# Two spectra kept in HBM in blocks of four frequencies: long runs for the stores, short runs for the loads

## The chip, the cores and the metric

The kernel runs on one NeuronCore of a Trainium2 chip. The metric is the device time of one execution in microseconds (us). A core has a matrix engine (PE, with its weight loads on PEld), a vector engine (DVE), an activation engine (ACT), a general engine (POOL), and a sync engine (SP) that issues nearly all DMAs here. PE reads SBUF and writes PSUM; only DMAs reach HBM. Sixteen DMA engines, which all queues share, carry the transfers.

## The reference

A long causal convolution by FFT over 8 sequences of 5696 tokens with 128 channels, followed by a mixture of 8 experts in which each token goes to one expert:

```python
L = 2 * S                                   # S = 5696
Xf = np.fft.rfft(x, n=L, axis=1)            # x: 8 x 5696 x 128
Hf = np.fft.rfft(h, n=L, axis=0)
y = np.fft.irfft(Xf * Hf[None], n=L, axis=1)[:, :S]
x = y.reshape(B * S, D)
logits = x @ w_gate                         # 8 experts
expert_idx = np.argmax(logits, axis=1)
probs = softmax(logits); gate_w = probs[expert_idx]
for e in range(E):                          # tokens of expert e
    out[mask] = gate_w[mask] * (relu(xe @ w1[e]) @ w2[e])
```

All of it is float32.

## The kernel before

The FFT is done in steps that are matrix products. The 8 sequences are split into three groups of 2, 3 and 3 (`SPLIT`). A group goes through three phases:

- **Phase A** (`steps_a`, line 296): the input `x` is multiplied by a small DFT matrix over one index (119 rows), and the result `U` (`ut`) goes to HBM, 6 KB per partition and store for groups 1 and 2.
- **Phase B** (`phase_b`, line 482): for each of 120 frequencies `q`, taken in 30 blocks of four, the block of `U` comes back (`uq`, two transfers of 48 x 4 runs of 1.5 KB), a 48-point transform `xp` runs on PE, DVE multiplies by the filter's spectrum `hh`, POOL or DVE adds, the inverse 48-point transform `vp` runs on PE, and ACT copies the result into `vt`. `ship` (line 640) stores `vt` into `V` in HBM, one transfer for the real and one for the imaginary half.
- **Phase C** (`phase_c`, line 782), "the sorts": for each of 24 slots of two columns `i`, `load` (line 806) brings `V` back as `vq` with the frequencies on the partitions (two transfers, one per half `k`), DVE forms sum and difference (`vr`, `divide`), PE finishes the inverse transform (`synth`, `yp`), the tokens are transposed (`tp`), the gate is computed, the token's rank within its expert is counted, and POOL scatters each row to its place in the sorted array `SR` by indirect DMAs.

The experts work on tiles of 256 sorted rows, `pipeline` (line 1448): a row load `xr`, two layers on PE (`mh` line 1328/1331 and `ma` line 1358/1363), and a scatter to `out`. The first 22 tiles use plain weights `wf` from the input; the later ones read weights that were split into two parts (`WD`, tiles `wb`). A weight load of a tile after the first ones of its part is conditional: it moves bytes only where the expert changes. Phase A of the next group runs inside phase C (`Guest`).

The order on each engine is written out by generators that are merged by planned costs (`run`, with `yield STEP * ...`), so the order is fixed when the program is built. SP takes its instructions strictly in that order: a DMA that waits holds back every DMA behind it. Each DMA of SP also uses one of eight completion semaphores in turn, and waits until the DMA eight places before it has landed.

`V` of a group is a DRAM array of rows (`2q + c`, column `i`, channel), made in `Group` (line 131). `by_frequency` (line 179) gives the view for one block of four frequencies. So a store writes, for each of 48 columns, four runs of 1.5 KB, and a load reads, for each of 128 rows, one run of 3 KB (two neighbouring columns). `LD` = 4 buffers of `vq` exist; slot n + 2 is loaded while slot n is worked on.

Of the kernel before, what the change touches and what calls it, by code (L numbers as in the profile page):

```python
# [23 lines left out]
NB = 48  # L24
MB = 119
QN = 2 * 60
# [5 lines left out]
PR = 128  # L32
# [52 lines left out]
def conv_moe(ctx: ExitStack, tc: tile.TileContext, I, out, B, S, D, E, F, split):  # L85
    nc = tc.nc
# [38 lines left out]
    class Part:  # L125
        def __init__(self, s, upto, tiles):
            self.s, self.upto, self.nt = s, upto, tiles
            self.sorted = self.tabled = self.filled = False
            self.lanes, self.fills = [], []
            self.since = self.known = 0  # L130
# [9 lines left out]
    class Group:  # L140
        def __init__(self, g, b0, nb):
            self.g, self.b0, self.nb = g, b0, nb
            self.cols = nb * D
            self.nch = -(-self.cols // 512)
            self.cb = nb // self.nch
            self.cw = self.cb * D
            assert self.cb * self.nch == nb
            self.ni = SLOTS[g] // nb
            while NB % self.ni:
                self.ni -= 1  # L150
            self.ns = self.ni * nb
            self.scb = 3 if self.ns % 3 == 0 else 2
            self.scw = self.scb * D
            self.qw = max(1, 512 // self.cols)
            self.qb = 4 if self.cols <= 384 else (3 if self.cols <= 512 else 2)
            rows = dram.tile([2 * QN + 2 * PR, NB, self.cols], F32, name=f"VU{g}")
            self.U = [rows[2 * QN + k * PR : 2 * QN + (k + 1) * PR] for k in range(2)]
            self.V = rows
            self.first = []

    groups, parts = [], []
# [2 lines left out]
    for g, nb in enumerate(split):  # L164
        gr = Group(g, b0, nb)
        gr.parts = []
        for upto in HALVES[g]:
            rows = sum(MB - (i + (MB - 1) * NB >= S) for i in ORDER[g][: upto * gr.ni])
# [7 lines left out]

    def by_frequency(gr, q, count, out):
        lo = 2 * (q % HQ)
        if out:
            rows = gr.V[2 * q : 2 * (q + count)]  # L180
        else:
            rows = gr.U[q // HQ][lo : lo + 2 * count]
        if gr.g:
            return rows.rearrange("(q c) i x -> c i q x", c=2)
        return rows.rearrange("(q c) i x -> (c i) q x", c=2)
# [26 lines left out]
    def part_of(width, rows=P):  # L212
        lo = taken[0]
        taken[0] += width
        return small[:rows, lo : lo + width]

    gcs = part_of(4 * MP, QN).rearrange("p (s k m) -> p s k m", s=2, k=2)
# [263 lines left out]
    def phase_b(gr, guest=None):  # L481
# [21 lines left out]
        def load_u(qb):  # L503
            q = qb * QB
            if q >= QN:
                return
            home, room = ("ld", LD) if g else ("mt", MT)
            uq = sb.tile([P if g else K2, QB, gr.cols], F32, tag=home, name=f"uq{g}_{q}", bufs=room)
            rows = by_frequency(gr, q, QB, False)
            for c in range(2 if g else 0):  # L510
                nc.sync.dma_start(uq[part_of_block(c)], rows[c])
            if not g:
                nc.sync.dma_start(uq, rows)
            tiles[qb] = uq
# [137 lines left out]
        def save(n):  # L652
            q, c = items[n]
            qb, k0 = divmod(q, QB)
            if k0 == 0 and c == 0:
                outs_[qb] = sb.tile([P if g else K2, QB, gr.cols], F32, tag="six", name=f"vt{g}_{q}", bufs=SIX)
            upto = HP + NB if g else K2
            dst = outs_[qb][:upto, k0 : k0 + QW, c * cw : (c + 1) * cw]
            nc.scalar.copy(dst, banks.pop(n)[:upto, : QW * cw].rearrange("p (j x) -> p j x", x=cw))  # L659
            if k0 + QW == QB and c == nch - 1:  # L660
                late.append((clock[0], by_frequency(gr, qb * QB, QB, True), outs_.pop(qb), qb))
                tiles.pop(qb), hhs.pop(qb), mats.pop(qb)
# [128 lines left out]
    def phase_c(gr, guest=None, after=None):  # L791
        g, nb, cb, cw, NI, ns = gr.g, gr.nb, gr.scb, gr.scw, gr.ni, gr.ns
# [14 lines left out]
        def load(n):  # L807
            if n >= nu:
                return
            if n < len(gr.first):  # L810
                vqs[n] = gr.first[n]
                return
            vq = sb.tile([PR, 2, NI, gr.cols], F32, tag="ld", name=f"vq{g}_{n}", bufs=LD)
            rows = gr.V[:, n * NI : (n + 1) * NI, :]
            for k in range(2):
                nc.sync.dma_start(vq[:, k], rows[k * QN : k * QN + PR])
            vqs[n] = [vq[:, k].rearrange("q i x -> q (i x)") for k in range(2)]

        nsub = ns // cb
# [4 lines left out]
        def bank(name, tag):  # L824
            return ps.tile([P, 512], F32, tag=tag if state["alone"] else "cx", name=name, bufs=banks[tag] if state["alone"] else 4)
# [14 lines left out]
        def synth(n, k):  # L840
            yp = bank(f"yp{g}_{n}_{k}", "mh")
            vr = vrs.pop((n, k)) if HALF3[g] else None
            for c in range(2):
                if HALF3[g]:
                    for j in range(c * HM, (c + 1) * HM, STRIP):
                        at = slice(j, j + STRIP)
                        done = nc.tensor.matmul(  # L847
                            yp[at, :cw], gcs[:, k, 0, at], vr[:, c], start=True, stop=True, tile_position=(0, j)
                        )
                else:  # L850
                    vk = vqs[n][c][:QN, k * cw : (k + 1) * cw]
                    done = nc.tensor.matmul(yp[:, :cw], gcs[:, 0, c], vk, start=c == 0, stop=c == 1)
            if k == nsub - 1 and not HALF3[g]:
                vqs.pop(n)
            ybank[n, k] = yp
            return done.ins
# [141 lines left out]
        for i in range(EARLY if guest and g == 0 else 0):  # L998
            if i == 0:
                for k in range(3):  # L1000
                    load(k)
            guest.begin(2)
            yield cost
            guest.end()
        for i in range(0 if guest and g == 0 else 2):
            load(i)
# [10 lines left out]
        for n in range(n_end + 1):  # L1017
            for k in range(nsub):
                at = n * nsub + k
                if parts[0].ready and (g or guest.m >= guest.M):  # L1020
                    state["alone"] = False
                if k == 0:
                    load(n + (2 if g else 3))
# [6 lines left out]
                if joint and k == 0:  # L1030
                    if n < nu:
                        made = [synth(n, j) for j in range(nsub)]
                    if 1 <= n <= nu:
                        for j in range(nsub):
                            spare = ybank.get((n, j))
                            if spare is None:
                                spare = bank(f"lp{g}_{n}_{j}", "mh")
                            read = logit(n - 1, j, spare)
                elif joint:
                    if n < nu:  # L1040
                        made = [turn(n, j, bank(f"tp{g}_{n}_{j}", "ma")) for j in range(nsub)]
                else:
                    if n < nu:
                        made = synth(n, k)
                    if TL <= at < total_sub + LL:
                        tp = bank(f"tp{g}_{n}_{k}", "ma")
                    if 0 <= at - TL < total_sub:
                        turning = turn(*divmod(at - TL, nsub), tp)
                    whole = 0 <= at - LL < total_sub and (at - LL) % nsub == nsub - 1
                    if whole:  # L1050
                        for j in range(nsub):
                            spare = tp if j else ybank.get((n, k))
                            if spare is None:
                                spare = bank(f"lp{g}_{n}_{k}", "mh")
                            read = logit((at - LL) // nsub, j, spare)
# [191 lines left out]
    rows, xts, accs, ots = {}, {}, {}, {}  # L1247
# [424 lines left out]
```

## Time and profile before

| What | Value |
|---|---|
| time, median of 3 runs | 2124.86 us (2123.58 to 2131.51) |
| profiled execution: device time | 2134.96 us |
| profiled execution: span | 2133.3 us |
| phase B of group 1 | about 390 to 675 us |
| phase C of group 1 | about 687 to 920 us |
| phase B of group 2 | about 985 to 1320 us |
| phase C of group 2 | about 1327 to 1580 us |

The span is what the profile shows between the first and the last instruction, and the device time has 1.7 us more around it. The profile's first part gives busy time per engine over the whole span; a matmul's end is modelled, so a busy PE is not a PE at its peak. The views used below are the busy time by stage (with the share of time in which the 16 DMA engines had a packet), the count of DMA packets of a stretch, the waits of one engine for another, the timeline, and the chain of waits that ended last. The stage bounds that the rows use lie inside the phases: 400 to 660, 690 to 900, 1000 to 1300 and 1350 to 1560 us.

### The profile page before, as it was taken

The numbers are of one execution on the slowest core, as the hardware profiler recorded it, in microseconds if no ns is written. First come the engines' busy times: TensorE is split into PE (matmuls) and PEld (weight loads), VectorE is DVE, ScalarE is ACT, GpSimd is POOL, SyncE is SP. The second block draws the span as 40 slices with busy tenths as digits, with TensorE's granted clock in tenths as the row PEclk, the third lists the DMA queues.
The fourth block names the chain that finished last, engine by engine and source line by source line (L and its number), as shares of the span: only waits on it lengthen the run. The fifth ranks groups of instructions, "written<-read, shape, count | busy, mean of one in ns | idle before, by whom it ended". The sixth has DMA issues, their size and how long they took to land.

```text
span 2133.3 us, 48456 instructions
## 1 busy us (share of the span) xinstructions
PE 1991.8 (93%) x15144; PEld 1547.0 (73%) x15144; DVE 1541.7 (72%) x3349; ACT 1043.5 (49%) x2243; POOL 1220.0 (57%) x1376
## 2 busy tenths in 40 slices
PE   9999888999998897889999999999998999999998
PEld 5788434555555464567666668888888999999998
DVE  6888656678884898867998987788875555555554
ACT  4788333455554343334555555444443444444444
POOL 2466266566563387875666655388885444444433
PEclk9999898999999998999999999999999999999999
DMA  9899985899997876757888897766654443433331
GB/s 362 274 294 293 356 280 199 209 259 273 265 271 245 312 258 231 251 173 195 220 219 234 223 253 217 261 221 226 222 164 158 143 145 127 131 124 120 132 122 33
DMA packets 233747, 463.82 MB, mean 217 GB/s; under 512 B 34034, under 2 KB 145271, under 8 KB 233488
## 3 DMA queue, kind: packets, MB, share of 16 engines
q1 hardware_dynamic: 209120, 412.40, 62.9%
q0 software_dynamic: 24368, 48.29, 6.9%
q8 instruction: 123, 2.02, 0.4%
q14 instruction: 136, 1.11, 0.2%
HBM read 551.67 MB, written 177.59 MB: 342 GB/s over the span
## 4 chain that ended last, share of the span: by engine, by line
PE 45%; issue 6%; DVE 6%; DMA 5%; POOL 2%; ACT 1%; SPq 1%; another core or an unknown queue 0%; POOLq 0%; DVEq 0%; ACTq 0%
PE mh L1331 17%; PE ma L1363 16%; DMA wb<-WD 3%; PE mx L207 3%; PE xp L583 2%; PE yp L847 2%; PE tp L207 2%; DVE hs L1344 1%; PE pa L331 1%; POOL out L1418 1%; DVE vr L835 1%; POOL SR L756 1%; DMA hh<-HS 1%; PE yp L895 1%; DVE ut L345 1%
## 5 line engine op out<-in xcount | busy, mean ns | idle before, releaser
L1344 DVE SCALAR_TENSOR_TENSOR hs<-mh,hs 128x512 fp32r<-128x512 f32 x640 | 439.8, 688 | 351.8 <-ACT hs L1342 269.4
L1331 PE MATMUL mh<-xtb,wb 128*128 128x256 f32 x3840 | 583.1, 288 | 23.5 <-DMA wb<-WD 9.9
L1342 ACT ACTIVATE hs<-mh 128x512 fp32r<-128x512 f32 x640 | 381.8, 597 | 434.4 <-PE mh L1331 327.9
L1331 PEld LDWEIGHTS mh<-xtb,wb 128*128 128x128 f32 x3840 | 503.3, 191 | 113.5 <-issue 44.5
L1363 PE MATMUL ma<-hs,wb 128*128 128x256 f32 x3840 | 578.3, 287 | 6.8 <-DMA wb<-WD 6.3
L756 POOL DMA_INDIRECT SR<-rt,pi x384 | 394.6, 1028 | 273.9 <-issue 82.0
L1363 PEld LDWEIGHTS ma<-hs,wb 128*128 128x128 f32 x3840 | 501.6, 191 | 8.3 <-DMA wb<-WD 7.2
L1418 POOL DMA_INDIRECT out<-xr x262 | 257.4, 982 | 330.3 <-DVE xr L1381 228.5
L609 POOL TENSOR_TENSOR zt<-zt,xs 128x384 f32<-128x384 f32 (+1 forms) x300 | 321.2, 1086 | 96.8 <-DVE xs L601 71.3
L659 ACT COPY vt<-vp 112x384 f32<-112x384 f32 (+1 forms) x300 | 150.2, 501 | 223.6 <-PE vp L627 212.1
L594 DVE TENSOR_TENSOR zt<-xp,hh 128x384 f32<-128x384 f32 (+1 forms) x300 | 173.9, 580 | 73.0 <-PE vp L627 29.0
L627 PE MATMUL vp<-zt,mt 48*64 48x384 f32 x960 | 206.4, 516 | 4.0 <-DVE xs L601 3.9
L583 PE MATMUL xp<-uq,mt 48*64 48x384 f32 x960 | 201.6, 511 | 0.1
L601 DVE SCALAR_TENSOR_TENSOR xs<-xp,hh 64x384 f32<-64x384 f32 (+1 forms) x300 | 175.8, 586 | 6.0
L1418 POOL DMA_INDIRECT out<-xb x102 | 99.7, 978 | 136.5 <-ACT ot L1373 88.5
L599 DVE TENSOR_TENSOR xs<-xp,hh 64x384 f32<-64x384 f32 (+1 forms) x300 | 173.2, 577 | 6.0
L345 DVE TENSOR_TENSOR ut<-ev,pa 128x512 f32<-128x512 f32 x192 | 122.2, 679 | 49.0 <-ACT ev L342 30.5
L331 PE MATMUL pa<-xt,c_fcs 64*128 64x512 f32 x384 | 126.4, 686 | 17.5 <-DVE xt L315 14.2
L750 POOL TENSOR_TENSOR c_fcs<-c_fcs 128x64 f32<-128x64 f32 (+1 forms) x288 | 115.1, 400 | 2.2
L835 DVE TENSOR_TENSOR vr<-vq 120x384 f32<-120x384 f32 x192 | 107.1, 599 | 2.2 <-DMA vq<-VU 2.2
L1328 PE MATMUL mh<-xtb,wf 128*128 128x256 f32 x352 | 100.9, 411 | 7.8 <-DMA wf<-moe_w 7.8
L1328 PEld LDWEIGHTS mh<-xtb,wf 128*128 128x128 f32 x352 | 62.0, 194 | 60.9 <-issue 36.1
(148 smaller groups left out, 2470.0 us busy)
## 6 DMA issues: line engine op xcount, KB each, us to landing
wb<-WD SPq DMA_DIRECT2D x640, 512.0 KB
vq<-VU SPq DMA_DIRECT2D x124, 384.0 KB
VU<-ut SPq DMA_DIRECT2D x48, 768.0 KB
uq<-VU SPq DMA_DIRECT2D x120, 288.0 KB
VU<-vt SPq DMA_DIRECT2D x120, 288.0 KB
xt<-x SPq DMA_DIRECT2D x96, 256.0 KB
xr<-SR SPq DMA_DIRECT2D x182, 130.0 KB
wf<-moe_w SPq DMA_DIRECT2D x88, 256.0 KB
```

What stands on the lines that cost most here:

```text
L583: nc.tensor.matmul(xj[to], lhs, uc[at], start=True, stop=True)
L594: nc.vector.tensor_tensor(out=zt, in0=x3, in1=hv[:, 0].broadcast_to([P] + wide), op=ALU.mult)
L599: nc.vector.tensor_tensor(out=xs[to], in0=x3[at], in1=him, op=ALU.mult)
L601: nc.vector.scalar_tensor_tensor(out=xs[to], in0=x3[at], scalar=-1.0, in1=him, op0=ALU.mult, op1=ALU.mult)
L609: eng.tensor_tensor(out=zt, in0=zt, in1=xs, op=ALU.add)
L627: nc.tensor.matmul(vj[to], mt[at, lo : lo + HP], zj[at], start=True, stop=True)
L756: s = nc.gpsimd.indirect_dma_start(out=SR[:, :], out_offset=IndirectOffsetOnAxis(ap=pi[:, b : b + 1], axis=0), in_=rt[:, b, :], in_offset= ...
L1331: nc.tensor.matmul(hp[:, u, :], wb[:, a, f, :], xt[:, b, :], start=(n == 0), stop=(n == 2))
L1342: done = nc.scalar.activation(hs[:, 0], hp, AF.Relu)
L1344: nc.vector.scalar_tensor_tensor(out=hs[:, 1], in0=hp, scalar=0.0, in1=hs[:, 0].bitcast(F32), op0=ALU.max, op1=ALU.subtract)
L1363: nc.tensor.matmul(accs[t], wb[:, a, f, :], hs[:, b, u, :], start=(k == 0 and u == 0 and n == 0), stop=(k == NPAIR - 1 and u == 1 and n == 2),
L1418: sc = nc.gpsimd.indirect_dma_start(out=out[:, :], out_offset=IndirectOffsetOnAxis(ap=xr[:, s, D + 1 : D + 2].bitcast(I32), axis=0), in_=x ...
```

## The change

`V` of groups 1 and 2 is viewed as blocks of four frequencies: block `b`, column `i`, place in the block, channel. A store of a block of four then writes, for each of 48 columns, one run of 6 KB. A load of a slot reads, for each column of the slot and each half, 32 blocks of four runs of 1.5 KB; it takes four transfers of 192 KB where there were two of 384 KB. Since a block of four rows now holds four frequencies of one part (real or imaginary) and not two frequencies of both, the rows of the matrix `gcs` that `synth` uses for groups 1 and 2 are put in that order on the host. Group 0 is as before.

```diff
             self.U = [rows[2 * QN + k * PR : 2 * QN + (k + 1) * PR] for k in range(2)]
             self.V = rows
+            flat = rows.rearrange("r i x -> (r i x)")
+            self.VB = flat.rearrange("(b i q x) -> b i q x", i=NB, q=self.qb, x=self.cols)
...
     def by_frequency(gr, q, count, out):
         lo = 2 * (q % HQ)
+        if out and gr.g:
+            b = 2 * q // gr.qb
+            return gr.VB[b : b + 2]
...
             vq = sb.tile([PR, 2, NI, gr.cols], F32, tag="ld", name=f"vq{g}_{n}", bufs=LD)
-            rows = gr.V[:, n * NI : (n + 1) * NI, :]
+            at = slice(n * NI, (n + 1) * NI)
             for k in range(2):
-                nc.sync.dma_start(vq[:, k], rows[k * QN : k * QN + PR])
+                if g:
+                    blocks = slice(k * QN // gr.qb, (k * QN + PR) // gr.qb)
+                    for j in range(NI):
+                        nc.sync.dma_start(vq[:, k, j], gr.VB[blocks, n * NI + j])
+                else:
+                    nc.sync.dma_start(vq[:, k], gr.V[k * QN : k * QN + PR, at])
...
                         done = nc.tensor.matmul(
-                            yp[at, :cw], gcs[:, k, 0, at], vr[:, c], start=True, stop=True, tile_position=(0, j)
+                            yp[at, :cw], gcs[:, 1, k, at], vr[:, c], start=True, stop=True, tile_position=(0, j)
                         )
...
+    blocked = np.arange(QN).reshape(QN // 8, 4, 2).transpose(0, 2, 1).reshape(-1)
+    gcs[:, 1] = gcs[blocked, :, 0]
```

On PE, DVE, ACT and POOL no instruction moves. On SP the stores keep their places, and 96 DMAs are added beside the 96 loads of `vq` of groups 1 and 2. The first place is SP in phase B of group 1, around one block of four frequencies, before:

```order
L493 DMA mt_72_6017<-mm 48x400 x2
L292 DMA WD<-wsp_882 128x1024
L511 DMA uq_72_6060<-VU_71 48x4x384 x2
L521 DMA hh_94<-HS 48x1024
L644 DMA VU_71<-vt_56_5924 48x4x384 x2
```

The same place after the change:

```order
L498 DMA mt_72_6017<-mm 48x400 x2
L297 DMA WD<-wsp_882 128x1024
L516 DMA uq_72_6060<-VU_71 48x4x384 x2
L526 DMA hh_94<-HS 48x1024
L649 DMA VU_71<-vt_56_5924 48x1536 x2
```

Only the shape of the store differs: 48 runs of 1536 numbers and not 48 x 4 runs of 384. The second place is SP in phase C of group 2, around the load of one slot, with the experts' weights `wb` and rows `xr` on either side, before:

```order
L1296 ISA
L1296 DMA wb_0_7972<-WD 128x1024
L816 DMA vq_22_22498<-VU_72 128x768 x2
L1296 ISA
L1296 DMA wb_1_7974<-WD 128x1024
L1296 ISA
L1296 DMA wb_2_7976<-WD 128x1024
```

And after the change:

```order
L1306 ISA
L1306 DMA wb_0_7982<-WD 128x1024
L824 DMA vq_22_22590<-VU_72 128x1x384 x4
L1306 ISA
L1306 DMA wb_1_7984<-WD 128x1024
L1306 ISA
L1306 DMA wb_2_7986<-WD 128x1024
```

Four DMAs of 128 runs of 384 numbers stand where two of 128 runs of 768 stood, and the weight loads `wb_1` and `wb_2` come behind them.

## Rows read from the trace of the kernel before

**Rows 1.** Busy time by stage: phases B, C of group 1, then of group 2.

```profile
core 0: us, PE busy (x) PEld busy (x) DVE busy (x) ACT busy (x) POOL busy (x), PEclk, DMA share, GB/s
400.00:660.00 260.00, 244.35 (x1541) 140.38 (x1540) 215.66 (x380) 136.55 (x266) 162.74 (x160) 0.98 0.95 258
690.00:900.00 210.00, 177.08 (x1413) 112.04 (x1412) 179.08 (x509) 79.62 (x223) 144.70 (x202) 0.90 0.77 262
1000.00:1300.00 300.00, 286.02 (x2332) 202.06 (x2328) 269.07 (x496) 164.39 (x306) 194.13 (x193) 0.98 0.85 235
1350.00:1560.00 210.00, 206.47 (x2026) 178.50 (x2025) 170.36 (x484) 99.86 (x275) 164.00 (x223) 1.00 0.67 219
```

**Rows 2.** Waits (us in total, times, longest), all engines, 400 to 660 us.

```profile
ACT hh L526 <- DMA hh<-HS: 6.1, 3, 3.6
PE ma L1358 <- DMA wf<-moe_w: 5.7, 2, 3.3
PE mh L1328 <- DMA wf<-moe_w: 5.6, 2, 3.9
```

**Rows 3.** Waits, all engines, 1000 to 1300 us.

```profile
PE mh L1331 <- DMA wb<-WD: 7.4, 4, 2.6
ACT hh L526 <- DMA hh<-HS: 6.1, 3, 3.0
PE ma L1363 <- DMA wb<-WD: 2.7, 2, 1.5
```

**Rows 4.** Waits, all engines, 690 to 900 us.

```profile
PE mxNone L207 <- DMA xr<-SR: 7.9, 2, 4.6
```

**Rows 5.** DMA packets and share of queue 1, 0 to 40 us.

```profile
DMA packets 5132, 14.65 MB, mean 366 GB/s; under 512 B 563, under 2 KB 563, under 8 KB 5131
q1 hardware_dynamic: 5131, 14.64, 96.6%
```

**Rows 6.** The same, 80 to 200 us.

```profile
DMA packets 26372, 35.94 MB, mean 299 GB/s; under 512 B 1814, under 2 KB 21294, under 8 KB 26360
q1 hardware_dynamic: 26360, 35.79, 99.3%
```

**Rows 7.** The same, 480 to 640 us, inside phase B of group 1.

```profile
DMA packets 24667, 43.12 MB, mean 269 GB/s; under 512 B 3025, under 2 KB 19505, under 8 KB 24650
q1 hardware_dynamic: 23818, 41.22, 94.1%
q0 software_dynamic: 832, 1.71, 3.8%
```

**Rows 8.** Timeline of SP, 560 to 600 us: start, us, instructions.

```profile
561.81 1.34 SPq L511 DMA_DIRECT2D uq<-VU  x2
...
598.60 0.93 SPq L511 DMA_DIRECT2D uq<-VU  x2
```

**Rows 9.** DMAs on `VU`: duration of the issue in ns, min/median/max.

```profile
L816 SPq DMA_DIRECT2D vq<-VU x124: 14/432/1614, 229.3 to 1552.6; - x124
L513 SPq DMA_DIRECT2D uq<-VU x30: 317/838/2581, 69.4 to 195.6; - x30
```

**Rows 10.** Waits of the SP queue (us in total, times, longest), 690 to 900 us.

```profile
SPq L322 <- DVE ut L345: 32.4, 14, 8.9
SPq L1296 <- PE mh L1331: 16.8, 4, 7.6
SPq L1296 <- remote: 8.8, 1, 8.8
```

**Rows 11.** Waits of the SP queue, 1350 to 1560 us.

```profile
SPq L1296 <- PE ma L1363: 29.1, 18, 3.2
SPq L1296 <- PE mh L1331: 15.6, 10, 2.4
```

**Rows 12.** The chain that ended last, 680 to 700 us.

```profile
688.28 4.42 DMA vq<-VU
...
695.30 1.13 PE pa L331 x4
```

## What I expect, worked out before the run

> **What bounds the kernel now.** I read the busy time by stage first, since the change touches four stretches: phases B and C of groups 1 and 2. PE is busy 244 of 260 us in B of group 1, 286 of 300 in B of group 2 and 206 of 210 in C of group 2 [rows 1]. It is the bound there, with 15.7, 14.0 and 3.5 us idle. In C of group 1 it is busy 177 of 210 us and DVE 179, so that neither bounds it alone. The DMA engines are what differs: 0.95 of the time they hold a packet in B of group 1, 0.85 in B of group 2, 0.77 and 0.67 in the two C [rows 1].
>
> Then the waits, to see how much of PE's idle time the DMAs make. In B of group 1 PE waits 5.7 + 5.6 = 11.3 us for expert weights [rows 2]; in B of group 2 it is 7.4 + 2.7 = 10.1 us [rows 3]. ACT waits 6.1 us in each for the filter `hh`. In C of group 1 PE waits 7.9 us for rows `xr` of the experts [rows 4]; in C of group 2 no engine has a wait for a DMA that the view shows. No wait on `V` itself stands in phase B. So the stores can gain only through what they leave to other transfers.
>
> **What one packet costs.** The page counts one packet per run. Between 0 and 40 us nearly all runs are long: 5132 packets of 2855 B on average, at a share of 0.968 (queue 1 and 0.2% of instruction fetches) [rows 5], so 40 x 16 x 0.968 / 5132 = 120.7 ns each. Between 80 and 200 us 26372 packets average 1363 B at 0.998, with 0.5% of instruction fetches counted [rows 6]: 72.7 ns. The line through both is 28.8 ns per packet and 0.0322 ns per byte. It gives 78 ns for 1.5 KB, 128 for 3 KB, 227 for 6 KB.
>
> In phase B itself packets are dearer: from 480 to 640 us 24667 packets of 1748 B at 0.982 (with 0.3% of fetches) take 101.9 ns [rows 7], where the line says 85.1. The excess is 16.8 x 24667 ns = 414 us of engine time. Four blocks take 598.6 - 561.8 = 36.8 us [rows 8], so this stretch holds 17.4 blocks, each with 768 runs of 1.5 KB (192 in each of its two loads and two stores), 13,400 in all. If they carry the whole excess, each costs 31 ns more: 109 ns. A 1.5 KB packet thus costs 78 to 109 ns here.
>
> **The stores.** 60 per group, each 192 runs before and 48 now: 11,520 packets become 2880. Four short ones cost 312 to 436 ns, a long one 227. What is saved is 85 to 209 ns, 2880 times, over 16 engines: 15 to 38 us of DMA time per group. I take 25, about the middle, since the stretch measured is the stage itself but loads `uq` with the same short runs share its excess. The share falls from 0.95 to 0.95 - 25/260 = 0.85 in B of group 1, and from 0.85 to 0.77 in B of group 2.
>
> By the Trainium skill ("DMA: Bandwidth & Descriptors", sections "Specifications" and "Why small descriptors are slow (HBM only)") this saving hardly exists: transfers of 512 B and more run at line rate, and a packet pays about 3 cycles beside one per 32 B, which is 51 cycles for 1.5 KB against 195 for 6 KB, so four short ones cost 4.6% more. By that page a group saves some 2.5 us of DMA time, an estimate, where I take 25. Two stretches of this trace speak against it, but their mixes of reads and writes differ too, so it stays a rival.
>
> What the share is worth, I read from the other stages: PE waits for DMAs 4.3% of the time at 0.95, 3.4% at 0.85 and not at all at 0.67 [rows 1 to 3]. B of group 1 at 0.85 would wait 3.4% of 260 = 8.8 us and not 11.3: a gain of 2.5. B of group 2 at 0.77 lies between: 3.4% x 0.10 / 0.18 = 1.9% of 300 = 5.7 us, a gain of 4.4. The waits for `hh`, 6.1 us each, fall in proportion (22% and 44%) by 4.0 us; half of that I let reach the end: 2.0. Bounds: nothing if these waits come from the order of requests and not from the load, and 11.3 + 10.1 + 6.1 = 27.5 us if all go. Taken: 8.9 us gained. After that PE's own work is next in both stages, with DVE at 216 of 260 and 269 of 300.
>
> **The loads.** 48 per group become 96: 24 slots with 256 runs of 3 KB become 512 of 1.5 KB. Two short ones cost 157 to 218 ns, one long 128: 29 to 90 ns more, 6144 times over 16, is 11 to 35 us of DMA time per group, and 48 x 16 completion packets of 29 ns add 1.4. Should the queue fetch the four neighbouring runs of a block as one, it is nothing. I take 15, near the lower end, as the excess was seen in B and not in C. The share goes from 0.77 to 0.84 in C of group 1 and from 0.67 to 0.74 in C of group 2. The first waits 7.9 us, 3.8%, at 0.77, and the B rows give 4.3% at 0.95: about 1 us more. For the second the line from 0.67 gives 1.3% of 210 = 2.8 us. Lost: 3.8.
>
> Phase C of group 1 starts on these loads: the chain goes from the issue to 4.42 us of `vq`, through `vr` to PE's `pa` [rows 12]. The first half of a slot needs the third DMA now (column 0 of either half) where it needed the second. One more issue costs 0.43 us at the median of `vq` and up to 1.65 us more for the three if each takes 0.838, the median of `uq` of group 0 [rows 9]; its bytes are fewer. I take 0.9 for group 1 and 0.5 for group 2, where PE has experts to work on. Lost: 1.4.
>
> **SP.** Each slot gets four issues where it had two. At 0.43 us each that is 0.86 us more; at 0.838, 4 x 0.838 - 2 x 0.432 = 2.49 us more. I take the nearest row, the same line's 0.43. Behind `vq` stand the conditional weight loads, the row loads, and in C of group 1 the loads of `x` for the guest. The cover is SP's own waiting. In C of group 2 it waits 29.1 + 15.6 = 44.7 us for PE to free weight buffers [rows 11], and the phase's 24 slots take some 253 us, so 210 us hold 20 of them: 2.2 us each. In C of group 1 it waits 32.4 + 16.8 + 8.8 = 58.0 us [rows 10], and 24 slots take some 233 us, so that is 2.7 each, but 1.2 without the 32.4 at the stores of `ut`. With 0.86 the cover holds: nothing. Without it, a rival below. As two slots are loaded ahead, a `vq` later by 1 to 2 us is not missed.
>
> PE's instructions are the same, with another slice of `gcs`: nothing.
>
> **The sum.** -8.9 + 3.8 + 1.4 + 0 (SP) = -3.7 us. On the profiled execution that is 2134.96 (span 2133.3 and 1.7 around it) to 2131.3. That execution lies 10.1 us above the median of the runs, so for the median it is 2124.86 - 3.7 = 2121.
>
> **Rivals.**
> 1. *The DMA engines pace both B.* For it: a share of 0.95, and SP's slow issues at such times. All 27.5 us go, the losses of 5.2 stay: 2124.9 - 22.3 = 2103. Against it: PE's whole idle time in both B is 29.7 us [rows 1], and some of it is waiting for DVE.
> 2. *SP becomes late in the sorts.* Place: SP behind each `vq`. Price at 0.838 per issue: 2.49 a slot against 2.2 in C of group 2 is 0.3 x 24 = 7 us; in C of group 1 it is nothing against 2.7 and 1.3 x 24 = 31 us against 1.2, say 15; the starts 3.3; contention 3.8; the gain of 8.9 stays. Sum +20: 2145. It decides from about 0.7 us per issue: the cover of C of group 1 ends between (1.2 + 0.86) / 4 = 0.52 and (2.7 + 0.86) / 4 = 0.89. For it: a form with more dimensions has the slow row. Against it: that row is from the stretch with a DMA share of 0.998 [rows 6], where a full queue holds issues back.
> 3. *Short runs are no dearer*, as that page has it: then the stores free next to nothing, some 0.9 us, and the loads cost their 5.2 at most: 2129, no change. The change then writes long runs to no effect.
>
> **How the numbers follow.** Forecast 0.40, first rival 0.23, second 0.15, third 0.22. This kernel's time can be told from no change beyond about 0.5%, or 10.6 us. Faster: the first rival's 0.21 of 0.23, and 0.07 of the forecast, where the waits fall further than the line says: 0.28. Slower: 0.10 of the second, 0.04 of the third and 0.04 of the forecast, where the C stages take the upper ends of 35 us: 0.18. The same: 0.54. The range goes from the first rival's 2103 to 2139, short of the second's 2145. The forecast's own is 2112 to 2131.
>
> **What would show it.** Right: the packets of 480 to 640 us fall by about 17.4 x 288 = 5000, the DMA share in both B falls by about 0.1, the waits for `wf`, `wb` and `hh` shrink, and the shares in both C rise by some 0.07. The issue of `vq` stays near 0.43 us, and SP's waits for PE in C of group 2 shrink by 0.9 us a slot without PE waiting. Wrong: `vq` issues at 0.7 us or more with new PE waits for `wb`, `xr` or `vr` in the sorts; an unchanged share in B; or a share that falls while PE's idle time in B stays, since the waits then hung on the order of the queue.

## The result: 0.9% slower, and on some chips only

The first comparison gave 2150.29 us (median of 7 runs, 2146.14 to 2156.92) against 2133.51 (median of 7): a ratio of 1.0092 (95% interval [1.007, 1.0115]), outside the predicted range. Five more comparisons, each on another chip, follow below. The change itself was timed again on four chips and gave 1.0003, 1.0015 and 1.001, all no change, and once more a loss, 1.0064.

The profiled execution of the first comparison took 2146.14 us, span 2144.4; its span is 11.1 us above that of the profile before, where the medians differ by 16.8. B1, C1, B2 and C2 stand below for phases B and C of groups 1 and 2. Busy time by stage after the change; the first four rows answer to [rows 1], the last is a stretch late in the experts, where nothing of the change is left:

```profile
core 0: us, PE busy (x) PEld busy (x) DVE busy (x) ACT busy (x) POOL busy (x), PEclk, DMA share, GB/s
400.00:660.00 260.00, 244.32 (x1528) 140.57 (x1522) 215.85 (x380) 136.82 (x265) 164.98 (x162) 0.98 0.93 263
690.00:900.00 210.00, 169.29 (x1375) 107.67 (x1364) 173.32 (x497) 76.71 (x218) 145.60 (x202) 0.89 0.75 250
1000.00:1300.00 300.00, 284.21 (x2312) 201.55 (x2310) 267.12 (x492) 163.97 (x303) 193.55 (x193) 0.98 0.84 234
1350.00:1560.00 210.00, 201.69 (x1964) 173.97 (x1955) 163.41 (x463) 96.63 (x265) 154.42 (x210) 0.99 0.67 215
1700.00:1760.00 60.00, 60.00 (x507) 59.05 (x507) 33.52 (x59) 28.34 (x57) 28.27 (x30) 1.00 0.46 156
```

In phase B the DMA share fell by 0.02 and 0.01 only, and PE idles as long as before, 15.7 and 15.8 us (15.7 and 14.0 before). In phase C the share did not rise, but PE does less in the same time: 7.8 us less in group 1 and 4.8 us less in group 2.

The DMAs from 480 to 640 us, against [rows 7]. The columns of the queue rows are packets, MB, share of 16 engines:

```profile
DMA packets 19495, 42.48 MB, mean 265 GB/s; under 512 B 3017, under 2 KB 12809, under 8 KB 19476
q1 hardware_dynamic: 18676, 40.62, 90.1%
q0 software_dynamic: 800, 1.64, 3.4%
```

The packets fell by 5172 (5000 were foretold) and the bytes by 1.5%, yet queue 1 only from 94.1% to 90.1%. The short runs were cheaper than I had them.

The waits of that stretch of B (first three rows, against [rows 2]) and of B of group 2 (the others, against [rows 3]); us in total, times, longest:

```profile
PE mh L1338 <- DMA wf<-moe_w: 10.3, 5, 4.1
...
ACT hh L531 <- DMA hh<-HS: 5.6, 3, 4.0
...
PE ma L1368 <- DMA wf<-moe_w: 0.8, 1, 0.8
...
ACT hh L531 <- DMA hh<-HS: 9.2, 3, 5.6
...
PE ma L1373 <- DMA wb<-WD: 4.4, 3, 1.6
...
PE mh L1341 <- DMA wb<-WD: 3.6, 2, 2.0
```

PE's waits for weights went from 11.3 to 11.1 (10.3 + 0.8) and from 10.1 to 8.0 us, ACT's for `hh` from 12.2 to 14.8 in all. The gain of 8.9 us is not there.

Where the 11.1 us between the two spans are can be read from the products `yp` of the sorts, the first and last of a group's 24 slots (us; "span" from first to last):

| profiled execution | start C1 | span C1 | C1 to C2 | span C2 | rest |
|---|---|---|---|---|---|
| before, first comparison | 696.4 | 231.1 | 407.6 | 237.6 | 560.6 |
| after, first comparison | 689.2 | 238.6 | 409.1 | 246.8 | 560.6 |
| the change, chip 14 | 691.5 | 237.0 | 411.1 | 252.1 | 559.6 |
| four_rows_2, chip 14 | 691.8 | 234.7 | 411.5 | 237.5 | 563.0 |
| the change, chip 2 | 666.8 | 225.2 | 404.2 | 233.7 | 540.8 |
| the change, chip 6 | 667.5 | 226.7 | 404.3 | 234.5 | 542.5 |
| the change, chip 10 | 665.4 | 222.3 | 398.5 | 234.0 | 541.3 |

C of group 1 starts 7.2 us earlier, of which 5.0 arise before the changed code (the first `vp` of group 1 is at 395.9 after 400.9). Then 7.5 us are lost in C1, 1.5 between, 9.2 in C2: -7.2 + 7.5 + 1.5 + 9.2 = 11.0, which is the 11.1 but for rounding.

The issue of `vq` (ns, min/median/max), against [rows 9]:

```profile
L824 SPq DMA_DIRECT2D vq<-VU x192: 295/602/2341, 679.7 to 1565.1; - x192
```

It takes 0.60 us and not 0.43. Four of them are 2.41 us a slot where two were 0.86: 1.55 us more, and not the 0.86 that I took. SP's waits from 1350 to 1560 us, against [rows 11]:

```profile
SPq L1306 <- PE ma L1373: 15.9, 16, 2.5
SPq L1306 <- PE mh L1341: 11.1, 8, 3.3
```

SP still waits 27.0 us there (44.7 before), and PE has no wait for a DMA in that stretch.

### The profile page after: what moved, and what is told of

It reads as the page before. It is cut to its first block, busy times and chain, and to the rows that moved or that the text cites. A ratio compares the mean times of both kernels' runs of the same rounds, so it can differ in the third digit from the quotient of the medians.

```text
span 2144.4 us, 48583 instructions
## 1 busy us (share of the span) xinstructions
PE 1992.2 (93%) x15144; PEld 1549.8 (72%) x15144; DVE 1544.3 (72%) x3349; ACT 1045.7 (49%) x2243; POOL 1224.1 (57%) x1376
## 4 chain that ended last, share of the span: by engine, by line
PE 49%; issue 7%; DMA 5%; DVE 4%; POOL 2%; SPq 1%; ACT 1%; another core or an unknown queue 0%; POOLq 0%; DVEq 0%; ACTq 0%
PE mh L1341 18%; PE ma L1373 17%; PE xp L588 3%; PE mx L212 3%; DMA wb<-WD 3%; PE yp L857 2%; PE tp L212 2%; PE pa L336 1%; POOL out L1428 1%; DMA SR<-rt,pi 1%; DMA xr<-SR 1%; PE yp L905 1%; DVE hs L1354 1%; POOL SR L761 1%; DVE vr L845 0%
## 5 line engine op out<-in xcount | busy, mean ns | idle before, releaser
L1428 POOL DMA_INDIRECT out<-xr x262 | 257.8, 984 | 332.4 <-DVE xr L1391 234.9
```

Source lines behind the costliest of these rows:

```text
L1428: sc = nc.gpsimd.indirect_dma_start(out=out[:, :], out_offset=IndirectOffsetOnAxis(ap=xr[:, s, D + 1 : D + 2].bitcast(I32), axis=0), in_=x ...
```

## The experiments

Theories at the start: (1) SP's time: the longer issues make the weight loads late; (2) the traffic: four short runs cost more than two; (3) the count of DMAs in the queue. The layout in HBM is a fourth. Kernels timed on one chip share its runs of the kernel before. The chips are numbered, since they turned out to matter; the first comparison's has no number.

**Chip 15: one suspected cost at a time.** Rows stored as before, but four loads per slot:

```diff
-                nc.sync.dma_start(vq[:, k], rows[k * QN : k * QN + PR])
+                for j in range(NI if g else 0):
+                    nc.sync.dma_start(vq[:, k, j], rows[k * QN : k * QN + PR, j])
+                if not g:
+                    nc.sync.dma_start(vq[:, k], rows[k * QN : k * QN + PR])
```

> V keeps the layout of before; groups 1 and 2 load each slot in four transfers of 128 runs of 1.5 KB (one per half and column), so the stores are as before and the loads have the count and the run length of the change, but their plain two-dimensional form. Theory 1 (SP time: what the change costs is that SP spends 4 x 0.602 - 2 x 0.432 = 1.54 us more per slot on issues, and about 20 us of time come from 48 slots of it): issues at 0.43 us, 0.86 us more per slot, so about 11 us slower (ratio 1.005). Theory 2 (short runs make the DMA traffic of the sorts dearer): the whole loss, ratio 1.009. Theory 3 (the count: only eight DMAs of SP can be in flight, and 96 more use places): the whole loss too, ratio 1.009.

The builder has a switch, `dge_precook`, that is on by default; with it off, the same two loads take 592 ns at the median to issue and not 432. The texts call the two forms short and slow. The two old loads in the slow form:

```diff
+                nc.dge_precook = not g
                 nc.sync.dma_start(vq[:, k], rows[k * QN : k * QN + PR])
+                nc.dge_precook = True
```

> Before, with the two loads per slot of groups 1 and 2 kept off the short form of issue by the builder's switch; the transfers, their count and their runs are unchanged. Issues of vq should take about 0.60 us and not 0.43. Theory 1: 0.34 us more per slot, about 4 us slower (ratio 1.002). Theories 2 and 3: no change (1.000).

The kernel before with four tiny DMAs more per slot:

```diff
+    tiny = [const.tile([16, 8], F32, name=f"tiny{k}") for k in range(8)]
...
+            for j in range(4 if g else 0):
+                nc.sync.dma_start(tiny[n % 2 * 4 + j], I["small"][:16, :8])
```

> Before, with four more DMAs per slot of groups 1 and 2, each of 16 runs of 32 B into tiles that nothing reads: SP time and places in flight without traffic. Theory 1: 4 x 0.33 to 0.43 = 1.3 to 1.7 us more per slot, 17 to 22 us slower (ratio 1.008 to 1.010). Theory 2: no change. Theory 3: four more DMAs per slot where the change has two, so up to twice the loss, ratio 1.009 to 1.018.

The kernel before with two register loads more per slot on SP:

```diff
+            for j in range(2 if g else 0):
+                nc.sync.value_load(parts[0].tab[0:1, 0, j : j + 1], min_val=0, max_val=E * CAP)
```

> Before, with two more register loads from SBUF on SP per slot of groups 1 and 2 (values that nothing uses), about 1 us each, in the place behind the two loads of vq: SP time alone, no DMA. Theory 1: some 2 us more per slot, about 25 us slower (ratio 1.008 to 1.013). Theories 2 and 3: no change (1.000).

Measured: four_rows 1.0006 [0.9985, 1.0027], slow_issue 1.0014 [0.9991, 1.0037], tiny4 1.0019 [0.9996, 1.0041], sp_busy 0.9995 [0.9975, 1.0015]. None made a loss that can be told from nothing. The register load of sp_busy, expected at about 1 us, took 0.59. All three theories were thereby hard to hold, but the change itself had not run on this chip.

**Chip 10: the change beside its parts.** First the change again, then four_rows in the slow form, which is SP's work in the change (600 ns per issue at the median, 602 in the change):

```diff
-                nc.sync.dma_start(vq[:, k], rows[k * QN : k * QN + PR])
+                nc.dge_precook = not g
+                for j in range(NI if g else 0):
+                    nc.sync.dma_start(vq[:, k, j], rows[k * QN : k * QN + PR, j])
+                nc.dge_precook = True
+                if not g:
+                    nc.sync.dma_start(vq[:, k], rows[k * QN : k * QN + PR])
```

Then two kernels that read `V` in another order than it was written in, so that its columns and frequencies are mixed. loads_only is the change with the old stores:

```diff
-        if out and gr.g:
+        if False:
```

stores_only is the change with the old loads:

```diff
-                if g:
+                if False:
                     blocks = slice(k * QN // gr.qb, (k * QN + PR) // gr.qb)
```

> The change once more, beside the others of this call. SP time alone, more DMAs alone and short runs alone each left the time unchanged within 0.4% in the runs so far, so what is left of the change is its layout in HBM (long stores, loads from blocks) and the sum of four loads in the slow form. If the loss is a property of the kernel: ratio 1.007 to 1.011, about 15 to 23 us. If it came from the chip or the hour: under 1.004.

> V in the layout of before; per slot of groups 1 and 2 four loads of 128 runs of 1.5 KB, each issued in the slow form (0.60 us): SP does exactly what it does in the change, and only the addresses in HBM differ from it. If the loss is SP's sum of four slow issues (1.54 us more per slot): the whole of it, ratio 1.007 to 1.011. If it is the layout: no change, within 1.003.

> The stores of the change (runs of 6 KB) with the two loads of before, which read V by rows; so what is computed after the load of V in groups 1 and 2 belongs to mixed columns and frequencies, with the same amount of work. If the loads carry the loss: the gain of the stores alone, 0 to 9 us faster (ratio 0.996 to 1.000). If the stores carry it: slower by 15 to 23 us (1.007 to 1.011).

> The loads of the change (four transfers per slot from blocks of four) with the stores of before, by rows; what is computed after the load of V in groups 1 and 2 belongs to mixed columns and frequencies, with the same amount of work. If the loads carry the loss: 15 to 25 us slower (1.007 to 1.012). If it needs stores and loads together, or the stores carry it: within 1.003.

Measured: after_again 1.0003 [0.998, 1.0026], slow_four 1.0015 [0.9993, 1.0038], loads_only 0.9996 [0.9969, 1.0023], stores_only 1.0116 [1.0086, 1.0147]. The last is no answer: with the mixed data three more expert tiles ran (3912 matmuls of `ma` where there are 3840), so only its stages compare, and C1 and C2 take 222.2 and 233.9 us, as in the change (222.3 and 234.0). The surprise was the first: the change cost nothing here. The medians were 2073.53 us and 2074.52 before, the latter 2.8% below the first comparison's.

**Chips 2 and 6: was the first result a matter of the chip?** The kernels after_third, slow_four_2 and loads_only_2 are those above, as are after_fourth, slow_four_3 and loads_only_3. New are sp_busy6 and sp_busy4, which are sp_busy with six and four register loads.

> The change a third time. On the chip of the first measurement it was 0.9% slower, on the chip of the last call equal (ratio 1.0003, 0.998 to 1.0026), where all kernels ran some 2.5% faster. If the loss hangs on the chip, this chip shows one of the two, and the kernels beside it tell the cause where it is the first. If it was no property of the change at all: within 1.003 again.

> As slow_four: rows in HBM as before, four loads per slot in the slow form, beside the change. Ratio like the change's if SP's issues or the count of DMAs make the loss; within 1.003 while the change is slower if the layout makes it.

> As loads_only (what is computed after the load of V in groups 1 and 2 belongs to mixed columns and frequencies, with the same amount of work), beside the change: like the change's ratio if its loads make the loss, within 1.003 if its stores do.

> Before, with six register loads on SP per slot of groups 1 and 2 behind the loads of vq, where sp_busy had two and was not slower: about three times the SP time of sp_busy, some 3 to 6 us per slot. If SP's cover in the sorts is 2.2 to 2.7 us per slot, as I read it, it ends here: 1 to 3 us per slot too many, 50 to 140 us slower (ratio 1.02 to 1.07). If SP has far more cover than its waits show: within 1.005.

> The change once more, beside kernels that hold only parts of it. The first measurement gave 1.009 with 238.6 and 246.8 us from the first to the last product of the sorts of groups 1 and 2 (231.1 and 237.6 before); two repeats on other chips gave 1.000 and 1.002 with 222 to 225 and 234 us. If the loss belongs to chips on which PE completes fewer matmuls in a given time (507 per 60 us in the expert stretch, against 517), it comes back here only where that rate is low: ratio 1.006 to 1.012 and sorts longer than before by 6 us or more. If it belongs to the kernel, 1.006 or more at any rate. If it was particular to that one measurement, 0.997 to 1.003 whatever the rate.

> The change's SP work alone: rows stored as before, four loads per slot, each with the slow form of issue (0.59 us at the median). By the theory that SP's time makes the loss: as after_fourth within 0.002, so 1.006 or more wherever that is slower. By the theory that the block layout of V in HBM makes it (the four frequencies of a row 1.5 KB apart in blocks of 6 KB): 0.998 to 1.002 even where after_fourth is slower.

> Stores in rows as before, loads addressed as in the change (the columns so loaded are mixed, so V is not the one that the reference has; the amount of work is the same). SP's work and the loads' addresses are the change's, the stores are not. Theory of the loads: as after_fourth within 0.002. Theory of the stores: 0.999 to 1.003, and the sort of group 1 starts 2 to 6 us later than in after_fourth.

> The kernel before with four register loads per slot on SP and nothing else. Two per slot gave 0.9995, six gave 1.011. If SP's cover ends at a fixed point between them and is lost linearly from there, 1.002 to 1.007; if the cover is the 2.2 us per slot that the waits of the sort of group 2 give, four loads of some 0.44 us each (1.8 us) are still free: 0.999 to 1.002.

Measured on chip 2: after_third 1.0015 [0.9993, 1.0037], slow_four_2 1.0006 [0.9982, 1.0029], loads_only_2 1.0027 [1.0008, 1.0047], sp_busy6 1.0111 [1.0081, 1.0141]. On chip 6: after_fourth 1.001 [0.9989, 1.0031], slow_four_3 1.0005 [0.9982, 1.0028], loads_only_3 1.0014 [0.9992, 1.0036], sp_busy4 1.0025 [1.0006, 1.0045]. The change again costs nothing that can be told from no change, and its SP work alone neither.

The two sp_busy kernels show where SP's cover ends. From one register load to the next SP takes 0.57 us at the median (three instructions of 269, 147 and 18 ns and the gaps between them). The whole block in C2 is 2.28 us a slot with four loads and 3.51 with six. SP's waits of sp_busy4 from 1350 to 1560 us, against [rows 11]:

```profile
SPq L1298 <- PE ma L1365: 21.1, 22, 2.6
SPq L1298 <- PE mh L1333: 13.2, 13, 1.7
```

The same of sp_busy6:

```profile
SPq L1298 <- PE ma L1365: 2.4, 2, 2.1
SPq L1298 <- PE mh L1333: 2.1, 4, 1.2
```

With four, 34.3 us of waiting are left and C2 takes 234.9 us, as without them (234.5 and 234.0 in the change and slow_four_3 on that chip); the whole time, 0.25% longer, is at the edge of what can be told. With six, 4.5 us are left, and PE waits for weights in that stretch:

```profile
PE mh L1333 <- DMA wb<-WD: 5.2, 3, 1.9
```

C2 takes 245.5 us then, 12 more than the 233.7 of the change on the same chip. So the cover in C2 ends between 2.28 and 3.51 us a slot, at some 3.0 if 12 us are spread over 24 slots (an estimate). That is of chips 2 and 6; the 2.2 that the prediction read from [rows 11] is not above it, and the change's 1.55 lies below either. C1, where the prediction read 2.7 us a slot, keeps its span with six (223.9 us). It starts 9.5 us later than in slow_four_2 (679.0 against 669.5), of which 5.1 arise before the added code.

**Chip 14: the loss comes back.** The change and four_rows once more:

> The change once more. Three repeats gave 1.0003, 1.0015 and 1.001, all where PE completed 517 matmuls per 60 us in the expert stretch. If the first 1.009 hangs on PE's rate, a run at 507 to 511 gives 1.006 or more with sorts 6 us longer; at 517, 0.999 to 1.003. If it was particular to that measurement, 0.997 to 1.003 at either rate.

> Rows stored as before, four loads per slot in the short form of issue: 1.0006 earlier. Both theories: 0.998 to 1.003 here too. Should the change be slower and this not, the difference lies in the slow form or the block layout, as no other part differs.

Measured: after_fifth 1.0064 [1.004, 1.0088], four_rows_2 1.0014 [0.9995, 1.0033]. So the loss is real, it goes with the chip as far as these five show, and four short loads per slot in the short form, with the old stores, don't make it. The medians are 2147.68 and 2137.18. The table above shows the difference in C2, 252.1 against 237.5 us. Busy time of the change there (columns as in the first fence):

```profile
1340.00:1570.00 230.00, 218.13 (x2070) 188.24 (x2063) 173.43 (x484) 101.97 (x279) 156.56 (x214) 0.98 0.67 214
...
1385.00:1395.00 10.00, 7.91 (x63) 7.57 (x65) 6.63 (x12) 4.46 (x12) 6.53 (x10) 0.83 0.56 204
...
1405.00:1415.00 10.00, 7.87 (x71) 7.22 (x64) 5.55 (x15) 3.13 (x10) 7.54 (x12) 0.83 0.45 136
...
1515.00:1525.00 10.00, 7.33 (x61) 6.94 (x53) 5.01 (x12) 2.51 (x8) 6.70 (x10) 0.83 0.39 121
```

And of four_rows_2:

```profile
1340.00:1570.00 230.00, 226.06 (x2207) 195.22 (x2206) 184.62 (x518) 109.75 (x300) 170.00 (x231) 1.00 0.70 222
...
1405.00:1415.00 10.00, 8.93 (x88) 7.70 (x87) 7.21 (x23) 4.43 (x12) 8.95 (x13) 1.00 0.50 143
```

PE idles 11.9 us in these 230 with the change and 3.9 without: 7.9 us. And in three stretches of 10 us the granted clock is 0.83: 3.4 us at 1.2 instead of 2.4 GHz, 1.7 us of work lost in each, 5.1 in all. The 13.0 us together are most of the 14.6. PE's waits with the change from 1350 to 1560 us:

```profile
PE mh L1341 <- issue: 2.7, 2, 2.2
PE mx L212 <- ACT ot L1383: 2.7, 1, 2.7
PE mx L212 <- issue: 2.1, 1, 2.1
```

Three stalls of 2.1 to 2.7 us, and a dip of the clock in each. One of them in the timeline of all engines (start, us, engine, line, what, idle before):

```profile
1512.88 0.34 SPq L1279 DMA_DIRECT2D xr<-SR  x1
1513.27 2.46 SPq L824 DMA_DIRECT2D vq<-VU  x4
...
1514.29 0.58 ACT L1352 ACTIVATE hs<-mh 128x512 fp32r<-128x512 f32 x1
...
1515.84 0.53 SPq L1404 DMA_DIRECT2D STG<-xr  x1
...
1516.68 0.86 PE L1341 MATMUL mh<-xtb,wb 128*128 128x256 f32 x6
...
1519.29 0.60 ACT L1352 ACTIVATE hs<-mh 128x512 fp32r<-128x512 f32 x1 [4.42 <-remote]
1519.30 1.68 SPq L1306 DMA_DIRECT2D wb<-WD  x2
...
1520.20 0.69 PE L212 MATMUL mx<-ident,ot 128*128 128x128 f32 x2 [2.67 <-ACT ot L1383]
```

SP issues its four `vq` and a store, and then waits; ACT waits for PE; both go on at the same instant, 1519.3, and PE a microsecond behind them. What came late was PE's signals, the updates of a semaphore by which it tells the others that a group of matmuls is done. The matmul groups `mh`, `ma` and `mh` before the stall run as ever, a matmul every 0.12 us, and end at 1516.1, 1516.8 and 1517.5. In the record of these updates, which the kept trace holds and no view prints, the three signals come at 1519.21, 1519.28 and 1519.36. SP's next issue (L1306) waits for a signal of PE too, so SP was not late, and late weights don't fit either: no matmul of these groups waits.

The first comparison has two such stalls, at 1403.9 and 1500.9 us (2.1 and 2.6 us), both behind issues of `vq` and a store; the clock falls behind the second of them only. In all five stalls the matmuls before run at their pace, PE's last signals come 0.9 to 1.8 us after the last matmul, and SP's next issue waits for them.

The same record tells the chips apart. On every chip, a signal of PE comes 13 or 14 ns after the profile's end of its matmul at the median. Counted are those that come over 0.3 us (over 1 us) after the last matmul that gives one:

| kernel | chip | C1 | C2 |
|---|---|---|---|
| before | first comparison | 55 (7) | 22 (2) |
| the change | first comparison | 49 (15) | 24 (8) |
| the change | 14 | 49 (12) | 42 (11) |
| four_rows_2 | 14 | 50 (5) | 25 (1) |
| slow_issue | 15 | 49 (6) | 11 (0) |
| the change | 2, 6 and 10 | 0 | 0 |

The other kernels on chips 2, 6 and 10 have none in C1 and C2 either. On the other chips the record lacks some 300 of PE's 2542 signals, so their counts are lower bounds. So late signals of PE are there on the slower chips whatever the kernel, and with the change, on the two where it ran, more of them are over 1 us late. Why they come late, the trace doesn't say. Two parts of the change are left as what brings the long ones on such a chip: four loads in the slow form of the issue, and the blocked layout. slow_four and loads_only, which would tell them apart, ran only on chips without the loss.

## Why the prediction was wrong, step by step

1. **The step that failed: the price of phase C of group 2, 2.8 us for the busier DMAs, 0.5 for the start and "SP 0".** It lost 9.2 us in the first comparison, and 14.6 against four_rows_2 on chip 14, in two and three stalls behind late signals of PE, with dips of the clock behind four of the five. No term had such stalls, and on chips 2, 6 and 10 there are none and no loss: 1.0003 to 1.0015. SP's own term was mis-sized: I took "the nearest row, the same line's 0.43", the issue took 0.60, and the term was 1.55 us a slot and not 0.86. "With 0.86 the cover holds: nothing" holds at 1.55 too: SP had 27.0 us of waiting left, and 2.28 us more a slot were free in sp_busy4. The second rival had the place (C of group 2, 7 us) and the total (2145, measured 2150) by luck: "from about 0.7 us per issue" is not what was seen, and SP waited for PE in the stalls and not PE for SP. What in the change makes the signals later stays open.
2. **The price of a short run was mis-sized.** I had 78 to 109 ns for 1.5 KB against 227 for 6 KB. Over all packets of the traces the medians are 65 ns for 1.5 KB, 121 for 3 KB, 159 for 4 KB and 234 for 6 KB: four short ones are 260 against 234, 11% more. By the Trainium skill ("DMA: Bandwidth & Descriptors", section "Why small descriptors are slow (HBM only)") it is 4.6%, an estimate from its 3 cycles per packet; the trace's medians are nearer to that than to my 37 to 92%. The medians lie on a line of some 8 ns per packet; my 28.8 came from two means over mixes of sizes that also hold delays. By the means, which the share counts, a block of four in 480 to 640 us took 768 x 99.4 ns before and 384 x 121.5 + 96 x 262.2 ns after: 4.5 us less, so 8.5 us per group over 16 engines, an estimate, where I took 25.
3. **So the gain of 8.9 us in B fell away**, by the third rival: share -0.02 and -0.01 where -0.10 and -0.08 were foretold. Beyond the 5.0 us that arise before it, C1 starts 2.2 us earlier. On chips 2, 6 and 10 the change takes from 1.2 us more to 4.3 us less from the first `vp` of group 1 to C1 than slow_four and loads_only, which store rows. That PE's waits follow the share, as read from one stage to another, was not borne out: in B of group 1 PE waited 11.1 us at 0.93 and 11.3 at 0.95, in B of group 2 8.0 at 0.84 and 10.1 at 0.85. The third rival's no change is what the change shows on these three chips.
4. **The loads' 3.8 us** were too high at their root: the share in C2 stayed at 0.67 where 0.74 was foretold, as two packets of 1.5 KB took 159 ns there at the mean and one of 3 KB 153. A loss of that size, 0.18%, can't be told: four_rows is at 1.0006 and 1.0014, with intervals of 0.2% to either side.
5. **C1** lost 7.5 us in the first comparison and 2.3 against four_rows_2. Its span moves by as much between executions of kernels that time alike (224.8 to 232.9 us on chip 15, sp_busy and slow_issue), so I don't read it.

Right were the count of packets, PE's unchanged work, and that SP's cover holds.

## What to carry to other kernels

A stage's DMA share is not a price per packet: take the duration of packets of each size from one stretch before you fit a line through two. Before a form of DMA is changed, find a row of the new form's issue, since its time on the queue changes with the access pattern and is multiplied by every issue. A ratio under 1% from one chip is a ratio of that chip: repeat it on another before it is explained. And where several engines stop and go on together, look for when the signals between them came before naming the one that the view of waits names.

## What the hardware showed unexpectedly

The chips differ, where the granted clock and the median from one matmul to the next (117 ns) are the same. The stretch 1700 to 1760 us of the change on chip 6, where the first fence has 507 matmuls at clock 1.00:

```profile
1700.00:1760.00 60.00, 60.00 (x517) 60.00 (x516) 33.73 (x61) 30.26 (x60) 28.68 (x30) 1.00 0.42 133
```

The part behind the last sort, the same work in all, takes 541 to 544 us on chips 2, 6 and 10, some 554 on chip 15 and 560 to 563 in the first comparison and on chip 14; the kernel before takes 2075, 2119 and 2131 to 2134 us. The loss of the change goes with the last group of chips. Over an execution, 170 to 245 signals of PE are over 0.3 us late on chips 14 and 15 and in the first comparison, and 2 or 3 on chips 2, 6 and 10. That these late signals are what makes the chips slower fits, but isn't shown.

The issue of a DMA of 128 runs on SP takes 432 ns at the median in one form (two loads before, four in four_rows) and 592 to 602 ns in the other (slow_issue, slow_four, the change), whether the run is of 3 or of 1.5 KB. And a stall of PE of 2 to 3 us can cost more than itself: behind four of the five, the clock falls to 1.2 GHz for 3.4 us, which is 1.7 us of work.
